# P transposes of three heads with 128 weight columns, and P, its transpose and the small columns in one tile

## The chip, the cores and the metric

The kernel runs on one core of a Trainium2 chip. A core has TensorE (matmuls into PSUM, with weight loads that are instructions of their own), VectorE (DVE), ScalarE (ACT), GpSimd (POOL) and SyncE (SP), which run their own instruction streams and meet through semaphores; DMA queues are filled by SP and POOL. The metric is the device time of one execution in microseconds, as a median over runs. Before the change it is 1793.92 us (three runs, 1793.05 to 1796.88).

## The reference

Two kinds of layer alternate, A, B, A, B, each added to its input after a layer norm. The sequence has 2048 rows of 512; A has 32 heads of 128.

```python
def _A_ref(x, mem0, Wq, Wk, Wv, Wo, seg_len):       # seg_len 32, M = 8 memory rows
    L = M + seg_len
    mask = (idx[:, None] < M) | (idx[:, None] >= idx[None, :])
    mem = mem0
    for s in range(n_seg):                          # 64 segments, one after the other
        h = jnp.concatenate([mem, xs], axis=1)      # 40 rows
        q, k, v = h @ Wq, h @ Wk, h @ Wv            # per head
        p = softmax(where(mask, q @ k.T * scale, -1e9))
        o = (p @ v) @ Wo                            # summed over heads
        mem = o[:, :M, :]                           # memory of the next segment
        outs.append(o[:, M:, :])
def _B_ref(x, w_gate, w_up, w_down):                # 512 -> 1792 -> 512
    return (sigmoid(x @ w_gate) * (x @ w_up)) @ w_down
```

Every segment of A needs the 8 memory rows that the segment before it produced, so A is a chain of 64 steps in each of the two layers.

## The kernel before

**Steps.** The two A layers run as one chain of 70 steps (`emit_step`). In step t, job 0 is segment t of the first A layer and job 1 is segment t - 6 of the second; where both exist (58 steps) the two 40-row segments lie side by side in 80 columns, `LW = 2 * L`. The B layers (`ffn`), the layer norms and the passes that make V run between the steps.

**Inside a step.** The 32 heads go in six groups: four of six heads, one of six and one of two. A "unit" is a set of heads whose P and V are stacked over partitions: the first eight units have three heads (3 x 40 = 120 partitions), the last four have two (80 partitions). So the first four groups have two units of three heads each, the fifth three units of two, the sixth one unit of two. For each group:

1. q and k of three heads at a time (L988, weights of 128 x 128, 80 moving columns), copied from PSUM to `qku` by ACT (L1354).
2. Scores (L1023); DVE adds the mask (L1037), takes the maximum (L1042), subtracts it (L1044); ACT takes the exponential (L1047); DVE sums (L1049), takes the reciprocal (L1051) and multiplies into `pb` (L1054), a bf16 tile of 80 partitions by 6 heads x 40.
3. P is transposed on TensorE, unit by unit (L1067): the weights are the unit's columns of `pb` (120 columns for three heads, 80 for two), the moving operand is the identity (80 columns), and the result lies in PSUM with the unit's heads stacked over 120 or 80 partitions.
4. Head i of each unit is copied ("spread") from PSUM rows 40 i to 40 i + 39 into its own 40 columns of `ptsb`, so that `ptsb` is block diagonal. For i = 0 it is a plain copy; for i = 1 and 2 the copy is multiplied by a column of ones and zeros, `third[i]`, which lies among the small columns. Each copy is on ACT or DVE, whichever the order chose: L1346 and L1354 on ACT, L1348 and L1356 on DVE. L1354 and L1356 are helper lines that make all plain copies of those engines.
5. P times V (L1096), weights `vsb`, moving operand `ptsb`; ACT copies the result to `otsb` (L1354); Wo (L1114) accumulates over the groups, and its first rows become the memory of the next step (L1127, L1132).

**Tiles.** There are three `pb` tiles and three `ptsb` tiles, used in turn. `small` is one tile of 61 float columns: statistics of the layer norms (`lns`), maxima and sums of the softmax (`mx`), the two columns `third` and a constant. In all, seven tiles. `pb` and `ptsb` are cleared once at the start by POOL (L652, L657).

**Order.** A planner (`Planner`) holds every piece of work as a task. The order of the tasks is written out in the file (`SEQUENCE`, and `TURNS` for the turns of `qku`); the planner walks it with estimated durations, puts each task on an engine and a PSUM bank, and the result is issued as it stands. The semaphore waits are not written by hand: the tile framework derives them from the accesses to each tile, and leaves out a wait that an earlier one on the same engine already implies. It makes waits between two engines, and also of an engine on its own earlier instructions. POOL's weight transfers of the B layers (L1208, L1209, L1233) and SP's transfers of V into `vsb` (L956, L968) are tasks of the same order.

Of the kernel before, what the change touches and what calls it, by code (L numbers as in the profile page):

```python
# [13 lines left out]
BF16 = mybir.dt.bfloat16  # L14
F32 = mybir.dt.float32
# [5 lines left out]
P = 128  # L21
MEM = 8
SEG = 32
L = MEM + SEG
LW = 2 * L
# [7 lines left out]
def fview(base, dims):  # L33
    return bass.AP(tensor=base.tensor, offset=base.offset, ap=[tuple(base.ap[0])] + [tuple(d) for d in dims])
# [497 lines left out]
class Kern:  # L532
# [43 lines left out]
    def setup_tiles(self):  # L576
        ctx, tc, nc = self.ctx, self.tc, self.nc
        D, DC, H, HG, F, FC, R = self.D, self.DC, self.H, self.HG, self.F, self.FC, self.R
        HE = H * P
        c = ctx.enter_context(tc.tile_pool(name="c", bufs=1))  # L580
        dr = ctx.enter_context(tc.tile_pool(name="dr", bufs=1, space=bass.MemoryType.DRAM))
        self.scr = [dr.tile([self.NSEG * XS, HE], BF16, name=f"scr{j}") for j in range(2)]
        self.wq = c.tile([P, DC, HE], BF16, name="wq_sb")
        self.wk = c.tile([P, DC, HE], BF16, name="wk_sb")
        self.wv = c.tile([P, DC, HE], BF16, name="wv_sb")
        self.wo = c.tile([P, H, D], BF16, name="wo_sb")
        cst = c.tile([P, P + 2 * L], BF16, name="cst")
        self.ident, self.maskb, self.mask1 = cst[:, 0:P], cst[:, P:P + L], cst[0:L, P + L:P + 2 * L]
        small = c.tile([P, 61], F32, name="small")
        self.negh = small[:, 60:61]  # L590
        self.third = [None, small[:, 58:59], small[:, 59:60]]
        self.lns = [small[:, 10 * i:10 * i + 10] for i in range(4)]
        self.mx = [small[:, 40 + 6 * i:46 + 6 * i] for i in range(3)]
        self.NV = 2
        self.hT = [c.tile([P, DC, 2 * L], BF16, name=f"hT{i}") for i in range(R)]
        self.qku = [c.tile([P, 3, 2, LW], BF16, name=f"qku{i}") for i in range(3)]
        self.vsb = {("A", i): c.tile([P, 2, 1024], BF16, name=f"vsb{i}") for i in range(self.NV)}
        self.vsb.update({("B", i): c.tile([P, 2, 512], BF16, name=f"vsb{self.NV + i}") for i in range(self.NV)})
        self.st = [c.tile([P, HG, L], F32, name=f"st{i}") for i in range(3)]
        self.pb = [c.tile([LW, HG, L], BF16, name=f"pb{i}") for i in range(3)]  # L600
        self.ptsb = [c.tile([P, 17 * L], BF16, name=f"ptsb{i}") for i in range(3)]
        self.otsb = [c.tile([P, HG, 2 * L], BF16, name=f"otsb{i}") for i in range(2)]
        self.hot = fview(self.otsb[1][:, 0, 0:1], [(1, P)])
        self.NX = 6
        self.xs = [c.tile([P, D], BF16, name=f"xs{i}") for i in range(self.NX)]
        self.xa = [c.tile([P, D], BF16, name=f"xa{i}") for i in range(2)]
        self.oxT = [[c.tile([P, DC, P], BF16, name=f"oxT{j}_{i}") for i in range(2)] for j in range(2)]
        self.xn = [c.tile([P, D], BF16, name=f"xn{i}") for i in range(2)]
        self.xnT = [c.tile([P, DC, P], BF16, name=f"xnT{i}") for i in range(1)]
        self.kx = c.tile([P, H, 2, NE], BF16, name="kx")  # L610
        self.xq = dr.tile([self.LAG * P, H * 2 * NE], BF16, name="xq")
        self.hff = [c.tile([P, FC, P], BF16, name=f"hff{i}") for i in range(1)]
        self.th = [c.tile([P, 2, P], F32, name=f"th{i}") for i in range(1)]
        self.xvf = [c.tile([P, DC, P], BF16, name=f"xvf{i}") for i in range(2)]
        self.xvl = [c.tile([P, DC, P], BF16, name=f"xvl{i}") for i in range(3)]
        self.vst = [c.tile([P, 512], BF16, name=f"vst{i}") for i in range(3)]
        self.sst = [c.tile([P, 2, 512], BF16, name=f"sst{i}") for i in range(1)]
        self.NG, self.ND = 3, 3
        self.wg = [c.tile([P, DC, 2 * P], BF16, name=f"wg{i}") for i in range(self.NG)]
        self.wu = [c.tile([P, DC, 2 * P], BF16, name=f"wu{i}") for i in range(self.NG)]  # L620
        self.wd = [c.tile([P, 2, D], BF16, name=f"wd{i}") for i in range(self.ND)]
        pp = ctx.enter_context(tc.tile_pool(name="ps", bufs=1, space=PSUM))
        self.bank = Pool([pp.tile([P, 512], F32, name=f"bank{i}") for i in range(8)], {"bg": 3, "v": 3}, psum=True)
        self.qkp = Pool(self.qku)
        self.vstp = Pool(self.vst)
        self.sstp = Pool(self.sst)
        self.bootp = Pool([fview(w[:, 0, 0:1], [(1, 1024)]) for w in self.wd + self.wg + self.wu])
        self.xnp = Pool(self.xn)
        self.thp = Pool(self.th)
# [281 lines left out]
    def emit_step(self, t):  # L911
        nc, pl = self.nc, self.pl
# [7 lines left out]
        pr = slice(0, ncol)  # L920
        npart = ncol
        nj = len(jobs)
        full = slice(0, LW)
# [9 lines left out]
        if load:  # L933
            for lo, hi in parts:
                w = NE * 2
                pl.add("SP", 430, lambda lo=lo, hi=hi, w=w: nc.sync.dma_start(out=fview(self.kx[:, lo, 0, 0:1], [(1, (hi - lo) * w)]),
                                                                             in_=self.xq[(t - LAG) * P:(t - LAG + 1) * P, lo * w:hi * w]),
# [5 lines left out]
        def s_all(B):  # L943
            return B[:, 0:6 * ncol].rearrange("p (h k) -> p h k", h=6)
# [5 lines left out]
        for j in jobs:  # L950
# [4 lines left out]
            for vh, i, h0, nh in slots if s or not j else ():  # L955
                pl.add("SP", 430, lambda j=j, row=L * i + row + lo, h0=h0, nh=nh, vh=vh, r0=s * XS + lo, nx=nx: nc.sync.dma_start(  # L956
                    out=self.vsb[vh][row:row + nx, j, :], in_=self.scr[j][r0:r0 + nx, h0 * P:(h0 + nh) * P]),
                    r=[("vd", j, b, q, kk) for q in range(lo // 8, (lo + nx) // 8) for kk in range(h0 // 4, (h0 + nh) // 4)] + ([("wo", self.H - 1)] if t == 0 else []),
                    w=[("vx", j, vh, i)], lat=2700.0, nb=nx * 256 * nh, slow=0.9)
# [13 lines left out]
        for g, (heads, us) in enumerate(self.groups):  # L973
            gsz = len(heads)
            hs = slice(0, gsz)
            SB = pl.buf(self.bank)
            for w0 in range(0, gsz, 3):
# [5 lines left out]
                def qk(uh=uh, nh=nh, pq=pq):  # L983
                    for i, h in enumerate(uh):
# [7 lines left out]
                       w=[pq])  # L992
# [21 lines left out]
                for lo, hi in parts:  # L1014
                    if save and pos == hi:
                        w = NE * 2
                        pl.add("SP", 430, lambda lo=lo, hi=hi, w=w: nc.sync.dma_start(out=self.xq[t * P:(t + 1) * P, lo * w:hi * w],
                                                                                     in_=fview(self.kx[:, lo, 0, 0:1], [(1, (hi - lo) * w)])),
# [9 lines left out]
            st, mx = self.st[gi], self.mx[gi]  # L1028
            sm = rs = mx
            bi = self.nxt("pb", 3)  # L1030
            pb = self.pb[bi]
            n = gsz * L
            for idx, j in reversed(list(enumerate(jobs))):
# [4 lines left out]
                    out=st[pj_, hs], in0=s_all(SB)[pj_, hs, L * idx:L * (idx + 1)],  # L1038
# [6 lines left out]
                out=st[pr, hs], in0=st[pr, hs], in1=mx[pr, hs].unsqueeze(2).to_broadcast([npart, gsz, L]), op=ALU.subtract),  # L1045
# [5 lines left out]
            pl.add("DVE", 110, lambda hs=hs, rs=rs, sm=sm: nc.vector.reciprocal(out=rs[pr, hs], in_=sm[pr, hs]), r=[("mx", gi)], w=[("mx", gi)])  # L1051

            def pmul(gsz=gsz, hs=hs, st=st, rs=rs, pb=pb):
                nc.vector.tensor_tensor(out=pb[pr, hs, 0:L], in0=st[pr, hs],  # L1054
                                        in1=rs[pr, 0:gsz].unsqueeze(2).to_broadcast([npart, gsz, L]), op=ALU.mult)

            pl.add("DVE", dve_ns(n), pmul, r=[("st", gi, 0), ("st", gi, 1), ("mx", gi)], w=[("pb", bi)])
            pi = self.nxt("ptsb", 3)
            ptsb = self.ptsb[pi]
            PB = pl.buf(self.bank)  # L1060
            nu = len(us)
            w = gsz // nu

            def ptr(nu=nu, w=w, pb=pb, PB=PB):
                pt = PB[0:w * L, 0:nu * LW // 2].bitcast(BF16)
                for ul in range(nu):
                    nc.tensor.transpose(out=pt[:, ul * LW:(ul + 1) * LW], in_=pb[full, w * ul:w * ul + w, :].rearrange("p i k -> p (i k)"),  # L1067
                                        identity=self.ident[full, full])

            pl.add("PE", nu * mm_ns(LW), ptr, r=[("pb", bi)], w=[PB])  # L1070
            for i in range(w):
                def spread(i=i, nu=nu, ptsb=ptsb, PB=PB):
# [56 lines left out]
        else:  # L1129
            for idx, j in wj:  # L1130
                m = SEG + MEM * j
# [288 lines left out]
```

## Time and profile before

| | |
|---|---|
| timed runs, median (range) | 1793.92 us (1793.05 to 1796.88) |
| profiled execution, its own time | 1789.87 us |
| its span, first to last instruction | 1788.0 us |
| granted TensorE clock | 0.999 |
| P transposes (L1067) | 840 matmuls; 560 with 120 weight columns, 280 with 80 |
| spreads on ACT | 477 (L1346) + 260 (L1354 into `ptsb`) |
| spreads on DVE | 223 (L1348) + 160 (L1356 into `ptsb`) |
| DMA traffic | 273.39 MB, mean 153 GB/s |

In the groups of the profile, a line gives the source line, the engine and operation, output and input tiles, shapes (partitions x elements, or contraction rows * weight columns for TensorE) and the count; then the busy time in us and the mean duration of one in ns; then the engine's idle time in us ahead of these instructions, with what ended most of it. "PE" is matmuls, "PEld" weight loads, which run beside matmuls. A duration of a matmul or load is that of one, with its way through the array; the next one starts long before its end. In a time line, a row gives the start and length in us, the engine, line and operation, the count that was merged, and in brackets the idle time before it and what released it. "SPq" is SP's queue.

### The profile page before, as it was taken

The numbers are of one execution on the slowest core, as the hardware profiler recorded it, in microseconds if no ns is written. First come the engines' busy times: TensorE is split into PE (matmuls) and PEld (weight loads), VectorE is DVE, ScalarE is ACT, GpSimd is POOL, SyncE is SP. The second block draws the span as 40 slices with busy tenths as digits, with TensorE's granted clock in tenths as the row PEclk, the third lists the DMA queues.
The fourth block names the chain that finished last, engine by engine and source line by source line (L and its number), as shares of the span: only waits on it lengthen the run. The fifth ranks groups of instructions, "written<-read, shape, count | busy, mean of one in ns | idle before, by whom it ended". The sixth has DMA issues, their size and how long they took to land.

```text
span 1788.0 us, 91153 instructions
## 1 busy us (share of the span) xinstructions
PE 1752.0 (98%) x39103; PEld 1512.2 (85%) x39311; DVE 1182.3 (66%) x4076; ACT 1179.3 (66%) x3243; POOL 578.6 (32%) x837
## 2 busy tenths in 40 slices
PE   9999999999999999999999999999999999999998
PEld 4588788888888898989888898889888888889886
DVE  3367676776677667766776677667766765667675
ACT  4667777766666666666666666666666766666564
POOL 5412132422333242323324231333325231333432
PEclk9999999999999999999999999999999999999999
DMA  9735354634555463545546454556546454554543
GB/s 340 255 98 141 106 162 131 188 106 141 156 165 159 132 191 109 159 127 166 158 133 194 137 154 111 148 161 167 157 128 197 116 149 120 161 155 135 165 137 100
DMA packets 144752, 273.39 MB, mean 153 GB/s; under 512 B 34306, under 2 KB 82314, under 8 KB 144346
## 3 DMA queue, kind: packets, MB, share of 16 engines
q0 software_dynamic: 56720, 183.22, 35.1%
q1 hardware_dynamic: 87626, 84.31, 16.7%
q8 instruction: 308, 5.05, 1.2%
q14 instruction: 98, 0.80, 0.1%
HBM read 221.78 MB, written 27.07 MB: 139 GB/s over the span
## 4 chain that ended last, share of the span: by engine, by line
PE 89%; ACT 3%; DVE 2%; issue 1%; SPq 1%; DMA 1%; POOL 0%; DVEq 0%; ACTq 0%; POOLq 0%
PE bank L988 32%; PE bank L1114 17%; PE bank L1216 10%; PE bank L902 7%; PE bank L778 6%; PE bank L1023 4%; PE bank L1096 4%; PE bank L1239 4%; PE bank L1067 2%; PE bank L738 1%; DVE st L1037 1%; PE bank L1340 1%; SPq L968 1%; ACT ptsb L1346 1%; PE bank L1184 1%
## 5 line engine op out<-in xcount | busy, mean ns | idle before, releaser
L988 PE MATMUL bank<-hT,wq_sb 128*128 128x80 bf16 (+3 forms) x8960 | 615.5, 198 | 1.2
L988 PE MATMUL bank<-hT,wk_sb 128*128 128x80 bf16 (+3 forms) x8960 | 615.2, 198 | 0.8 <-issue 0.8
L1354 ACT CAST qku<-bank 128x480 bf16<-128x480 f32 (+3 forms) x770 | 380.7, 507 | 215.5 <-PE bank L988 185.1
L988 PEld LDWEIGHTS <-wq_sb 128*128 128x128 bf16 x8960 | 453.4, 99 | 23.3 <-issue 11.7
L988 PEld LDWEIGHTS <-wk_sb 128*128 128x128 bf16 x8960 | 447.0, 99 | 1.0 <-issue 1.0
L1037 DVE TENSOR_TENSOR st<-bank,cst 40x240 f32<-40x240 f32 (+3 forms) x768 | 278.9, 368 | 163.3 <-PE bank L1023 152.6
L1114 PE MATMUL bank<-otsb,wo_sb 128*128 128x80 bf16 (+1 forms) x8960 | 358.6, 198 | 1.6 <-ACT otsb L1354 0.2
L1114 PEld LDWEIGHTS <-wo_sb 128*128 128x128 bf16 x8960 | 336.5, 99 | 13.5 <-issue 0.9
L1209 POOL DMA_DIRECT2D wu<-in_B_w_up_dram x217 | 164.0, 756 | 273.6 <-PE bank L1216 126.5
L1208 POOL DMA_DIRECT2D wg<-in_B_w_gate_dram x217 | 163.9, 756 | 256.4 <-PE bank L1216 181.9
L1354 ACT CAST otsb<-bank 128x480 bf16<-128x480 f32 (+3 forms) x420 | 198.3, 483 | 52.3 <-PE bank L1096 35.4
L1233 POOL DMA_DIRECT2D wd<-in_B_w_down_dram x217 | 153.7, 709 | 207.4 <-PE bank L1023 71.8
L1346 ACT ACTIVATE ptsb<-bank,small 80x160 bf16<-80x160 bf16 (+5 forms) x477 | 169.5, 379 | 27.7 <-PE bank L1067 23.9
L1047 ACT ACTIVATE st<-st 80x240 f32<-80x240 f32 (+3 forms) x420 | 159.7, 383 | 29.0 <-DVE st L1044 25.6
L728 POOL TENSOR_TENSOR small<-small 128x1 f32<-128x1 f32 (+1 forms) x80 | 44.8, 563 | 402.1 <-DVE small L727 400.0
L1216 PE MATMUL bank<-xnT,wg 128*128 128x128 bf16 (+2 forms) x1784 | 172.0, 219 | 0.6
L1216 PE MATMUL bank<-xnT,wu 128*128 128x128 bf16 (+2 forms) x1784 | 171.0, 218 | 0.0
L1049 DVE TENSOR_REDUCE small<-st 80x6 f32<-80x240 f32 (+3 forms) x420 | 151.2, 362 | 24.5 <-ACT st L1047 22.8
L1023 PE MATMUL bank<-qku 128*128 128x80 bf16 (+1 forms) x2240 | 165.4, 198 | 0.7
L1044 DVE TENSOR_TENSOR st<-st,small 80x240 f32<-80x240 f32 (+3 forms) x420 | 154.4, 369 | 3.4
L1054 DVE TENSOR_TENSOR pb<-st,small 80x240 bf16<-80x240 f32 (+3 forms) x420 | 153.8, 369 | 4.2
L1042 DVE TENSOR_REDUCE small<-st 80x6 f32<-80x240 f32 (+3 forms) x420 | 151.8, 363 | 4.3
(104 smaller groups left out, 2405.3 us busy)
## 6 DMA issues: line engine op xcount, KB each, us to landing
wg<-in_B_w_gate_dram POOLq DMA_DIRECT2D x220, 256.0 KB, 4.4
wu<-in_B_w_up_dram POOLq DMA_DIRECT2D x220, 256.0 KB, 4.4
wd<-in_B_w_down_dram POOLq DMA_DIRECT2D x220, 256.0 KB, 4.3
vsb<-scr SPq DMA_DIRECT2D x345, 48.0 KB
vsb<-sst SPq DMA_DIRECT2D x372, 32.0 KB
scr<-vst SPq DMA_DIRECT2D x112, 96.0 KB
vsb<-scr SPq DMA_DIRECT2D x230, 24.0 KB
wv_sb<-in_A_Wv_dram SPq DMA_DIRECT2D x8, 512.0 KB
```

The lines of the kernel that those rows point to most:

```text
L988: nc.tensor.matmul(o_ap, lhsT=W[:, c, h * P:(h + 1) * P], rhs=mv(c), start=(c == 0), stop=(c == DC - 1))
L1023: nc.tensor.matmul(s_all(SB)[:, w0 + i, :], lhsT=fview(qku[:, i, 0, 0:1], [(1, P)]), rhs=qku[:, i, 1, 0:ncol], start=True, stop=True)
L1037: pl.add("DVE", dve_ns(n, True), lambda gsz=gsz, hs=hs, st=st, SB=SB, pj_=pj_, npj_=npj_, mk=mk, idx=idx: nc.vector.tensor_tensor(out=st[p ...
L1044: pl.add("DVE", dve_ns(n), lambda gsz=gsz, hs=hs, st=st, mx=mx: nc.vector.tensor_tensor(out=st[pr, hs], in0=st[pr, hs], in1=mx[pr, hs].uns ...
L1047: pl.add("ACT", act_ns(n), lambda hs=hs, st=st: nc.scalar.activation(out=st[pr, hs], in_=st[pr, hs], func=ACTF.Exp, scale=self.scale), r=s ...
L1054: nc.vector.tensor_tensor(out=pb[pr, hs, 0:L], in0=st[pr, hs], in1=rs[pr, 0:gsz].unsqueeze(2).to_broadcast([npart, gsz, L]), op=ALU.mult)
L1114: nc.tensor.matmul(WB[:, c * ncol:(c + 1) * ncol], lhsT=self.wo[:, h, c * P:(c + 1) * P], rhs=otsb[:, hl, 0:ncol], start=(h == 0 and c == ...
L1208: pl.add("POOL", 760, lambda wg=wg, fs=fs: nc.gpsimd.dma_start(out=wg[:], in_=self.wgv[:, :, fs]), r=[("wo", self.H - 1)], w=[gk] + bt, la ...
L1209: pl.add("POOL", 760, lambda wu=wu, fs=fs: nc.gpsimd.dma_start(out=wu[:], in_=self.wuv[:, :, fs]), r=[("wo", self.H - 1)], w=[uk] + bt, la ...
L1216: nc.tensor.matmul(gu[:, 2 * i + k, 0:n], lhsT=W[:, c, i * P:(i + 1) * P], rhs=xnT[:, c, rw], start=(c == 0), stop=(c == DC - 1))
L1346: nc.scalar.activation(out=dst, in_=src, func=ACTF.Copy, scale=by)
L1354: nc.scalar.copy(out=dst, in_=src)
```

## The change

The weights of a three-head transpose take 128 columns of `pb` in place of 120. The first unit's extra 8 columns are the first 8 of the second unit; the second unit's are 8 columns past the end of the P tile, which is now 248 columns wide and cleared at the start. The transpose writes 128 rows of PSUM, of which the last 8 are read by nothing. Transposes of two heads stay at 80 columns.

The three P tiles, the three `ptsb` tiles and `small` become parts of one tile, `pbt`: first the three `ptsb` of 680 columns, then the three P of 248, then the 61 float columns. The names `pb`, `ptsb`, `mx`, `lns`, `third` now are views of it. The planner's tasks, costs and written order are the same. In the changed file the lines from the tiles on stand 2 or 3 further down (the transposes at L1070, the spreads at L1349, L1351, L1357 and L1359).

```diff
-        small = c.tile([P, 61], F32, name="small")
-        self.negh = small[:, 60:61]
-        self.third = [None, small[:, 58:59], small[:, 59:60]]
-        self.lns = [small[:, 10 * i:10 * i + 10] for i in range(4)]
-        self.mx = [small[:, 40 + 6 * i:46 + 6 * i] for i in range(3)]
...
-        self.pb = [c.tile([LW, HG, L], BF16, name=f"pb{i}") for i in range(3)]
-        self.ptsb = [c.tile([P, 17 * L], BF16, name=f"ptsb{i}") for i in range(3)]
+        np_, nt_ = HG * L + P - 3 * L, 17 * L
+        pbt = c.tile([P, 3 * (np_ + nt_) + 2 * 61], BF16, name="pbt")
+        self.ptsb = [pbt[:, nt_ * i:nt_ * (i + 1)] for i in range(3)]
+        self.pb = [pbt[0:LW, 3 * nt_ + np_ * i:3 * nt_ + np_ * (i + 1)] for i in range(3)]
+        small = pbt[:, 3 * (np_ + nt_):3 * (np_ + nt_) + 2 * 61].bitcast(F32)
+        self.negh = small[:, 60:61]
+        self.third = [None, small[:, 58:59], small[:, 59:60]]
+        self.lns = [small[:, 10 * i:10 * i + 10] for i in range(4)]
+        self.mx = [small[:, 40 + 6 * i:46 + 6 * i] for i in range(3)]
...
             def pmul(gsz=gsz, hs=hs, st=st, rs=rs, pb=pb):
-                nc.vector.tensor_tensor(out=pb[pr, hs, 0:L], in0=st[pr, hs],
+                nc.vector.tensor_tensor(out=pb[pr, 0:gsz * L].rearrange("p (h k) -> p h k", k=L), in0=st[pr, hs],
...
             def ptr(nu=nu, w=w, pb=pb, PB=PB):
-                pt = PB[0:w * L, 0:nu * LW // 2].bitcast(BF16)
+                m = P if w == 3 else w * L
+                pt = PB[0:m, 0:nu * LW // 2].bitcast(BF16)
                 for ul in range(nu):
-                    nc.tensor.transpose(out=pt[:, ul * LW:(ul + 1) * LW], in_=pb[full, w * ul:w * ul + w, :].rearrange("p i k -> p (i k)"),
+                    nc.tensor.transpose(out=pt[:, ul * LW:(ul + 1) * LW], in_=pb[full, w * L * ul:w * L * ul + m],
                                         identity=self.ident[full, full])
```

## The prediction

> **What bounds the kernel now.** I read the page's busy rows, its chain that ended last, then groups of instructions with shapes kept apart, and last the time lines of single engines around one transpose.
>
> ```profile
> span 1788.0 us, 91153 instructions
> PE 1752.0 (98%) x39103; PEld 1512.2 (85%) x39311; DVE 1182.3 (66%) x4076; ACT 1179.3 (66%) x3243; POOL 578.6 (32%) x837
> ...
> PE 89%; ACT 3%; DVE 2%; issue 1%; SPq 1%; DMA 1%; POOL 0%; DVEq 0%; ACTq 0%; POOLq 0%
> ```
>
> TensorE sets the end: 89% of the last chain is its matmuls, and it idles for 1788.0 - 1752.0 = 36 us. So a matmul slot saved is time saved, unless TensorE then stands before an operand. ACT and DVE are two thirds busy, but they stand between TensorE's own steps. The rows of the changed transposes, with their peers:
>
> ```profile
> L988 PE MATMUL bank<-hT,wq_sb 128*128 128x80 bf16 x6656 | 485.7, 202 | 1.1
> ...
> L1096 PEld LDWEIGHTS <-vsb 120*128 120x128 bf16 x1024 | 65.5, 98 | 15.7 <-issue 4.6 <-DMA vsb<-sst 0.3
> L1067 PEld LDWEIGHTS <-pb 80*120 80x120 bf16 x560 | 55.7, 134 | 9.6 <-DVE pb L1054 1.9 <-DVE st L1044 0.4
> ...
> L1096 PEld LDWEIGHTS <-vsb 80*128 80x128 bf16 x512 | 28.9, 98 | 5.5 <-issue 1.0 <-DMA vsb<-scr 0.2
> L1067 PEld LDWEIGHTS <-pb 80*80 80x80 bf16 x280 | 22.2, 118 | 4.2 <-DVE pb L1054 0.9
> ...
> L738 PEld LDWEIGHTS <-xn 128*128 128x128 bf16 x312 | 19.8, 98 | 8.4 <-DVE xn L729 3.2 <-issue 2.1 <-DVE sst L1356 0.4
> ```
>
> The reader is to see the mean of one weight load: 118 ns with 80 columns, 134 with 120, but 98 with 128. It is 98 with 80 rows (vsb) as with 128, and in a transpose too (xn). Now the two time lines of ACT and DVE, where the change adds waits:
>
> ```profile
> 903.45 0.40 DVE L1049 TENSOR_REDUCE small<-st 80x6 f32<-80x240 f32 x1 [0.47 <-ACT st L1047]
> 903.89 0.19 DVE L1051 RECIPROCAL small<-small 80x6 f32<-80x6 f32 x1
> 904.11 0.41 DVE L1054 TENSOR_TENSOR pb<-st,small 80x240 bf16<-80x240 f32 x1
> ...
> 904.91 0.50 DVE L1348 TENSOR_SCALAR ptsb<-bank,small 120x160 bf16<-120x160 bf16 x2
> 905.33 0.22 DVE L1356 COPY ptsb<-bank 40x160 bf16<-40x160 bf16 x1
> ```
>
> ```profile
> 915.87 0.28 ACT L1354 COPY ptsb<-bank 40x160 bf16<-40x160 bf16 x1 [0.32 <-PE bank L1067]
> 916.06 0.67 ACT L1346 ACTIVATE ptsb<-bank,small 120x160 bf16<-120x160 bf16 x2
> ```
>
> The sum, reciprocal and product each read the one before and wait for it: each starts 0.03 to 0.04 us after its predecessor's end. The spreads wait for none of their own engine: the DVE copy starts at 905.33, 0.08 before the pair ahead ends (905.41), and ACT's pair starts at 916.06, 0.09 before the copy ends (916.15).
>
> **Part 1, the wider transposes.** 560 of the 840 P transposes change (groups of six heads; the 280 with 80 columns do not). Nothing is added or removed on TensorE: the built programs hold 78,624 rows in the same order, and only the output's 120 partitions become 128. In the trace, the first of two such transposes is followed by the second after 47.9 ns in the mean (283 pairs), and the second by the next matmul after 50 to 54 (45 or 55 each, where nothing stalls; 51 taken). Matmuls of 80 columns on weights of 128 follow each other after 35.8 (23,234 pairs, almost all 35 or 36). The saving is 280 x (47.9 - 35.8) + 280 x (51 - 35.8) = 3.4 + 4.3 = 7.6 us of TensorE's slots. It is all on the bound engine, but where TensorE stands before a wait afterwards it is given back. I carried the shorter slots forward through the trace's rows (every instruction starts when its engine is free and its semaphores have come, with the durations and least gaps of these rows; the rest stays as recorded): 7.3 us are won and 2.0 go back, about half of them before DMA-filled vsb (L1096), the rest before pb (L1067), qku (L1023) and otsb (L1114). The part is worth **-5.3 us**. From below: nothing, if the fast load is not taken; from above -7.6.
>
> The Trainium skill (TensorE: Matmul & The Clock Gate, LDWEIGHTS and Weight-path perf modes) has a load at columns / 1.2 ns, and about twice as fast with exactly 128 non-fp32 columns. By it the estimate is 560 x (100 - 53) = 26 us saved; the spacing of 48 to 51 ns that the rows show for 120 columns contradicts its 100, and the rows decide.
>
> **Part 2, one tile for P, its transpose and the small columns.** Same instructions on ACT, DVE and SP in the same order, and no wait between two engines changes. But the waits of an engine on itself do. In the built program of before, a spread (L1346, L1348, or the copy into ptsb at L1354 and L1356) is free of its neighbour. In the changed one, 255 spreads on ACT wait for the ACT instruction just ahead, nearly always the group's previous spread, and 81 on DVE likewise; 41 and 19 more wait for the one before that, which is over by then, and cost nothing. What it costs:
> - DVE: instructions without such a wait start 75 to 80 ns before their predecessor's end, with it 34 ns after (125 pairs L1037 to L1042, 111 pairs L1051 to L1054). 34 + 78 = 112 ns, and 81 x 112 = 9.1 us of DVE.
> - ACT: spread after spread starts 102 ns before the end (96 pairs L1346 to L1346). No ACT instruction of before waits for its direct predecessor closely enough to show the price. From below: it starts as the predecessor ends, 102 ns. From above: the largest gap between a producer's end and its consumer here, ACT to TensorE, 50 ns, so 152. Nearest are DVE to itself (34), DVE to ACT (33) and ACT to DVE (31); I take 34, so 136 ns, and 255 x 136 = 34.7 us of ACT.
> - Given back: 171 separate wait instructions on ACT vanish, because later instructions need not repeat the wait (76 on copies to otsb). A copy behind such an instruction starts up to 92 ns after TensorE's end, without it 37. This is within the sum below.
>
> Of 43.8 us on the two engines only what arrives late at TensorE counts. P·V (L1096) is first: in 338 of its groups, the spread was there for a median of 253 ns before it had to be, but for under 105 in a quarter. 161 groups get a longer chain of spreads, by one or two of these prices. Held against each group's own margin, 49 of them come late by 4.9 us together. That is the first order alone. Queued behind the spreads on ACT are the copies to otsb (Wo, L1114, waits), to qku (scores, L1023) and the exponentials (L1047, whose sum and product DVE makes for L1067); DVE's own next steps lie behind its spreads. Carried forward in the same way, with 34 ns on both, ACT's waits alone give +9.9 us, DVE's alone +2.0, both +11.9. Together with part 1 TensorE stands longer by 8.6 at L1096 behind spreads, 3.1 at L1114, 3.0 at L1067, 2.5 at L1023, and 1.1 before DMA-filled vsb; it wins 7.3 by spacing and about 3.5 because a stall leaves later ones shorter; with 0.4 of small ones, **+7.9 us**. With ACT and DVE at 50 ns it is +12.2, at 0 ns +2.2.
>
> The Trainium skill (VectorE: DVE Perf Modes, The DRAIN you can't avoid) holds that between chained DVE operations "the semaphore costs nothing extra here". By that sentence the sum would be part 1 alone, -5.3 us. The time line above shows 34 ns after the end against 78 before it, so the measurement decides for a price.
>
> **What has one answer.** The three memsets of pb get 8 of 240 columns more (301 ns each, so 10 ns, in the first 7 us, POOL off the chain): nothing. POOL's weight transfers and SP's keep their order and waits; POOL's wait for TensorE (181.9 us of it before wg) and move with it. The output in PSUM rows 120 to 127 is read by none.
>
> **The sum.** The profiled execution took 1789.87 us for a span of 1788.0; + 7.9 = 1797.8. The median of the three timed runs is 1793.92, 4.05 higher, so I forecast 1793.92 + 7.9 = **1801.8 us**. About 0.2% (3.6 us) either way can't be told from no change.
>
> **Rivals.**
> - *The waits hide and the slots are kept (faster).* For it: ACT idles a third of the time, and TensorE's recorded idle before L1096 for ACT's ptsb is small. Against it: a quarter of the margins at L1096 is under 105 ns, less than one wait's price. -5.3 gives 1788.6. It decides from an own-engine price of about 80 ns (start 20 ns before the end), where the carried sum crosses zero; below that it is faster.
> - *The change doesn't do what it says.* The second transposes start 240 bytes into a P tile, and the tiles now lie 496 bytes apart; every 128-column load of the trace starts at a rounder address. If the load stays slow, +11.9 and 1805.8 remain; with 128/120 of the slow slot, 560 x 3.3 ns = 1.9 more, 1807.7.
> - *No visible change.* Price about half: sum between -3.6 and +3.6, 1790 to 1797.5.
> - *The waits cost more.* At 60 ns after the end the carried sum is +16.8, 1810.7; stalls grow faster than the price, since more margins are used up.
>
> **How the numbers follow.** Chances: the likeliest, 0.48; waits hidden 0.17; slow load 0.10; no visible change 0.13; dearer waits 0.12. Slower is 0.48 + 0.10 + 0.12 = 0.70, same 0.13, faster 0.17. The likeliest alone spans 1798 to 1806 (price 15 to 50 ns). The range reaches from 1790, which keeps "no change" and leaves most of "faster" out, to 1811, the dearer waits.
>
> **What would show it.** After the change: the weight load of L1067 at about 98 ns instead of 134 and the two transposes in 0.07 us instead of 0.12; spreads that start 0.03 us after the one ahead instead of 0.08 to 0.10 before it; more idle of TensorE before L1096 put down to ACT's and DVE's ptsb (before: 0.6 + 0.2 us in its waits), and before L1114 and L1067. I am wrong if spreads still overlap, if the load stays over 130 ns, or if both hold but idle of TensorE doesn't grow.

## The result

The changed kernel took 1797.64 us in the median (20 runs), the kernel before 1793.07 beside it (20 runs): 1.0031 times as long, or 5.5 us more (95% intervals [1.0021, 1.0041] and [3.8, 7.4]). Differences in us are taken from such ratios unless it says otherwise; the two medians alone give 4.6. A second series gave 1.0027 [1.0012, 1.0042]. The forecast was 1801.8 us, +7.9, in a range of 1790 to 1811: the direction is right, and the size too large, by 2.4 us in the difference and by 4.2 in the time.

**The profile after.** Busy rows and the chain that ended last, from the page of the changed kernel:

```profile
span 1798.9 us, 91186 instructions
...
PE 1765.5 (98%) x39311; PEld 1504.5 (84%) x39311; DVE 1189.3 (66%) x4076; ACT 1197.1 (67%) x3243; POOL 578.8 (32%) x837
...
PE 87%; ACT 4%; SPq 2%; DMA 2%; DVE 1%; issue 1%; POOL 0%; DVEq 0%; ACTq 0%; POOLq 0%
```

TensorE's share of the last chain went from 89% to 87%, ACT's from 3% to 4%. ACT has the same 3,243 instructions, but is busy for 17.8 us more (1179.3 before), because instructions that used to overlap now follow each other. PE's own busy row must not be compared: the trace of before lacks 208 matmul records (39,103 of 39,311), this one none. Nor does it show TensorE's standing: the changed kernel idles for 1798.9 - 1765.5 = 33 us by this row, less than the 36 of before, because a record of about 200 ns covers several slots of 36. Single executions also scatter by several microseconds (those of before in one series lie between 1790.5 and 1802.4), so the 10.9 us between the two profiled spans are no measure of the change; the medians are.

Weight loads with shapes kept apart (count, busy us, mean ns of one, then idle time ahead), and the matmuls of the changed transposes:

```profile
L1099 PEld LDWEIGHTS <-vsb 120*128 120x128 bf16 x1024 | 66.9, 97 | 28.6 <-issue 14.0 <-DMA vsb<-sst 2.4 <-DVE pbt L1351 0.2
...
L1070 PEld LDWEIGHTS <-pbt 80*128 80x128 bf16 x560 | 40.4, 99 | 11.6 <-DVE pbt L1056 3.4 <-DVE st L1046 0.4
...
L1070 PEld LDWEIGHTS <-pbt 80*80 80x80 bf16 x280 | 22.2, 118 | 4.6 <-DVE pbt L1056 1.9
```

```profile
L1070 PE MATMUL bank<-cst,pbt 80*128 80x80 bf16 x560 | 66.2, 200 | 0.8 <-DVE pbt L1056 0.7
```

The load of a three-head transpose takes 99 ns in place of 134, and that of the unchanged 80-column transpose 118 as before. TensorE's time line at one such place, first before, then after:

```profile
904.58 0.29 PE L1067 MATMUL bank<-cst,pb 80*120 80x80 bf16 x2
904.70 0.28 PE L1023 MATMUL bank<-qku 128*128 128x80 bf16 x3
904.82 0.31 PE L988 MATMUL bank<-hT,wq_sb 128*128 128x80 bf16 x4
```

```profile
909.32 0.24 PE L1070 MATMUL bank<-cst,pbt 80*128 80x80 bf16 x2
909.39 0.27 PE L1025 MATMUL bank<-qku 128*128 128x80 bf16 x3
909.50 0.31 PE L990 MATMUL bank<-hT,wq_sb 128*128 128x80 bf16 x4
```

From start to start the two transposes take 0.07 us in place of 0.12, and the three score matmuls behind them 0.11 in place of 0.12. So the first half of the change does what it says. The second half shows in the idle time ahead of the P·V loads: 28.6 us in place of 15.7. It also shows in the time lines of ACT and DVE (start and length in us), here around the same work that the prediction quoted of before:

```profile
920.60 0.29 ACT L1357 COPY pbt<-bank 40x160 bf16<-40x160 bf16 x1 [0.26 <-PE bank L1070]
920.92 0.81 ACT L1349 ACTIVATE pbt<-bank,pbt 120x160 bf16<-120x160 bf16 x2
```

```profile
909.16 0.41 DVE L1225 SCALAR_TENSOR_TENSOR hff<-th,bank 128x256 bf16<-128x256 f32 x1
909.60 0.63 DVE L1351 TENSOR_SCALAR pbt<-bank,pbt 120x160 bf16<-120x160 bf16 x2
910.26 0.23 DVE L1359 COPY pbt<-bank 40x160 bf16<-40x160 bf16 x1
```

ACT's pair now starts at 920.92, 0.03 after the copy ends (920.89). Before, it started 0.09 ahead of that end. The pair itself takes 0.81 in place of 0.67, since its second spread waits for its first. DVE's pair takes 0.63 in place of 0.50, and the copy behind it starts 0.03 after its end in place of 0.08 before.

Over all spreads that follow another directly, counted in the traces (start minus the predecessor's end, median):

| | before | after, with the new wait | after, without one |
|---|---|---|---|
| ACT | -102 ns | +32 ns (255 cases, 31 to 33) | -102 ns |
| DVE | -77 ns | +35 ns (81 cases, 33 to 36) | -77 ns |

**Where TensorE stands.** Its waits in the changed kernel (us in total, times, longest); of the P·V lines, all are shown that have 0.5 us or more:

```profile
PE bank L1099 <- DMA vsb<-sst: 4.4, 5, 1.7
...
PE bank L1099 <- ACT pbt L1349: 2.4, 3, 1.8
PE bank L1099 <- issue: 2.0, 2, 1.2
PE bank L1099 <- DMA vsb<-scr: 1.7, 2, 0.9
...
PE bank L1117 <- ACT otsb L1357: 0.9, 3, 0.5
PE bank L1070 <- DVE pbt L1056: 0.7, 2, 0.4
PE bank L1099 <- ACT pbt L1357: 0.5, 2, 0.3
```

```profile
PEld L1099 <- issue: 15.4, 30, 1.9
...
PEld L1070 <- DVE pbt L1056: 5.3, 20, 0.5
...
PEld L1099 <- DMA vsb<-sst: 2.4, 3, 0.9
```

The largest entry, 15.4 us before P·V's loads (5.6 before), has no releaser: "issue" is waiting for nothing that this view shows. To name it I took each place where two weight loads start over 70 ns apart and asked which result, of all that the built program makes this load or the matmul just ahead of it wait for, came last. Where ACT or DVE had finished it less than 130 ns earlier, the gap, less a regular slot of 36 ns, is put down to them:

| TensorE behind ACT's and DVE's results, us (gaps) | before | after | change again | waits only | 128 columns only |
|---|---|---|---|---|---|
| P·V, behind spreads | 4.0 (22) | 16.3 (74) | 15.5 (75) | 15.5 (71) | 5.0 (23) |
| Wo, behind `otsb` (ACT) | 3.5 (24) | 6.9 (38) | 7.2 (39) | 6.8 (37) | 4.0 (27) |
| transposes, behind P (DVE) | 6.2 (28) | 10.0 (49) | 10.1 (49) | 9.3 (45) | 6.9 (32) |
| scores, behind `qku` (ACT) | 7.1 (35) | 9.4 (49) | 9.5 (51) | 8.7 (46) | 7.4 (35) |
| sum | 20.8 | 42.6 | 42.3 | 40.3 | 23.3 |

The last two columns are experiments below. The change adds some 21 us of such standing, over half of it before P·V, where it falls on about 50 more gaps. The growth of "issue" before P·V in the waits view, 9.8 us, fits into the 12.3 us found there; no other cause for it was seen, but the two were not matched gap by gap.

The table leaves out P·V's waits for V. By the waits view, the matmuls and loads of P·V wait for the transfers into `vsb` for 2.7 us in the kernel before and 8.9 in the changed one (8.1 in the second run). The same sum is 4.6 with the waits only, 5.1 with 128 columns only, 2.0 in the layout control below, and 7.3 with 124 columns, which has neither the waits nor the shorter slots. So this growth can't be put down to the change with any certainty.

### The profile page after: what moved, and what is told of

It is laid out like the page before. It is cut to its first block, busy times and chain, and to the rows that moved or that the text cites. A ratio compares the mean times of both kernels' runs of the same rounds, so it can differ in the third digit from the quotient of the medians.

```text
span 1798.9 us, 91186 instructions
## 1 busy us (share of the span) xinstructions
PE 1765.5 (98%) x39311; PEld 1504.5 (84%) x39311; DVE 1189.3 (66%) x4076; ACT 1197.1 (67%) x3243; POOL 578.8 (32%) x837
## 4 chain that ended last, share of the span: by engine, by line
PE 87%; ACT 4%; SPq 2%; DMA 2%; DVE 1%; issue 1%; POOL 0%; DVEq 0%; ACTq 0%; POOLq 0%
PE bank L990 31%; PE bank L1117 16%; PE bank L1219 9%; PE bank L904 7%; PE bank L780 6%; PE bank L1242 5%; PE bank L1099 4%; PE bank L1025 4%; SPq L970 2%; PE bank L1070 2%; ACT pbt L1349 2%; DMA vsb<-sst 1%; DMA vsb<-scr 1%; PE bank L740 1%; PE bank L1343 1%
## 5 line engine op out<-in xcount | busy, mean ns | idle before, releaser
L1357 ACT CAST qku<-bank 128x480 bf16<-128x480 f32 (+3 forms) x770 | 380.4, 507 | 209.9 <-PE bank L990 177.3
L1357 ACT CAST otsb<-bank 128x480 bf16<-128x480 f32 (+3 forms) x420 | 197.8, 482 | 55.7 <-PE bank L1099 39.7
L1349 ACT ACTIVATE pbt<-bank,pbt 80x160 bf16<-80x160 bf16 (+5 forms) x477 | 177.7, 381 | 29.0 <-PE bank L1070 19.9
L730 POOL TENSOR_TENSOR pbt<-pbt 128x1 f32<-128x1 f32 (+1 forms) x80 | 45.0, 564 | 403.7 <-DVE pbt L729 401.7
L1051 DVE TENSOR_REDUCE pbt<-st 80x6 f32<-80x240 f32 (+3 forms) x420 | 151.6, 363 | 31.8 <-ACT st L1049 28.7
L1046 DVE TENSOR_TENSOR st<-st,pbt 80x240 f32<-80x240 f32 (+3 forms) x420 | 154.6, 370 | 3.4
L1056 DVE TENSOR_TENSOR pbt<-st,pbt 80x240 bf16<-80x240 f32 (+3 forms) x420 | 153.9, 369 | 4.2
L1044 DVE TENSOR_REDUCE pbt<-st 80x6 f32<-80x240 f32 (+3 forms) x420 | 151.9, 363 | 4.3
```

The costliest lines, as they stand in the source:

```text
L1046: pl.add("DVE", dve_ns(n), lambda gsz=gsz, hs=hs, st=st, mx=mx: nc.vector.tensor_tensor(out=st[pr, hs], in0=st[pr, hs], in1=mx[pr, hs].uns ...
L1056: nc.vector.tensor_tensor(out=pb[pr, 0:gsz * L].rearrange("p (h k) -> p h k", k=L), in0=st[pr, hs], in1=rs[pr, 0:gsz].unsqueeze(2).to_broa ...
L1349: nc.scalar.activation(out=dst, in_=src, func=ACTF.Copy, scale=by)
L1357: nc.scalar.copy(out=dst, in_=src)
```

## The experiments

**The theory.** Two opposite effects of known place: the 128-column loads shorten TensorE's slots, and the new waits of ACT and DVE on themselves make TensorE stand behind spreads; the second is larger. **Rivals:** the loads bring nothing; the time comes from the new placement of the tiles in memory, not from waits; only one of the two engines matters; or the two parts do not add.

How the waits arise was seen in the built programs. With `ptsb` and the float columns in one tile, the 255 and 81 waits are there; with P and the float columns in one tile, or with `ptsb` and P in one tile and the float columns in another, there are none, and the waits between engines are the same in all. Of these three, only the last was also run, below. So one part can be had without the other.

**The change again**, beside the next three on the same chip. No edit.

> The changed kernel once more, beside the parts that are taken from it. Measured 1.0031 of before. Theory (the engines' waits on themselves cost more than the faster weight loads save): again 1.002 to 1.005, and the parts below add up to it. Rival (the layout of the one tile costs it): the same here, but the narrow kernel with the small columns apart is slower too.

Measured: 1801.73 us against 1796.03, ratio 1.0027 [1.0012, 1.0042]. The result repeats.

**The waits alone.** One tile as in the change, the transposes at 120 columns:

```diff
-                m = P if w == 3 else w * L
+                m = w * L
```

> One tile pbt as in the change, but the transposes take 120 columns again: the waits of ACT and DVE on themselves without the faster loads. Theory: +8 to +12 us over before (the carried sum had +11.9), ratio 1.0045 to 1.0067, weight loads at 134 ns. Rival 1 (the loss comes from the earlier transposes, which bring TensorE to V that is still on its way): about 0, ratio 1.000. Rival 2 (the layout): the same as the change, 1.003.

Measured: 1805.87 us, ratio 1.0058 [1.0039, 1.0078], or +10.4 us. The load is back at its old mean:

```profile
L1070 PEld LDWEIGHTS <-pbt 80*120 80x120 bf16 x560 | 55.5, 134 | 10.1 <-DVE pbt L1056 2.8 <-DVE st L1046 0.4
```

Without the wider transposes the changed kernel would be slower still. The standing behind ACT and DVE is 40.3 us, nearly that of the full change: it comes with the tile, not with the columns.

**The 128 columns alone.** The float columns stay a tile of their own; `ptsb` and P share one, so P lies where the change puts it:

```diff
-        pbt = c.tile([P, 3 * (np_ + nt_) + 2 * 61], BF16, name="pbt")
+        pbt = c.tile([P, 3 * (np_ + nt_)], BF16, name="pbt")
+        small = c.tile([P, 61], F32, name="small")
...
-        small = pbt[:, 3 * (np_ + nt_):3 * (np_ + nt_) + 2 * 61].bitcast(F32)
```

> The transposes take 128 columns, P and its transpose share one tile, and the small float columns are a tile of their own again. In the built program no engine waits more than before. Theory: the saving alone, -3 to -6 us, ratio 0.9967 to 0.9983; spreads overlap again by about 100 ns on ACT and 77 on DVE. Rival 1 (earlier transposes only move the wait to V): 1.000 or above. Rival 2 (layout of P and its transpose in one tile): 1.002 or above.

Measured: 1789.59 us, ratio 0.9958 [0.9940, 0.9975], or -7.5 us (-6.4 by the medians): faster than both kernels, and by somewhat more than the 3 to 6 us expected. Both rivals wanted 1.000 or more: that the earlier transposes only move the wait to V does not hold. It ran again in the next series:

> The kernel with the small columns apart once more, beside the two that add waits to it. Measured 0.9958 of before. Both theories: 0.995 to 0.998.

Measured: 1788.41 against 1795.79, ratio 0.9956 [0.9941, 0.9972], -7.9 us. Its loads (by shapes) are the short ones, and its spreads (time line of ACT) overlap again:

```profile
L1070 PEld LDWEIGHTS <-pbt 80*128 80x128 bf16 x560 | 40.8, 99 | 11.0 <-DVE pbt L1056 2.3 <-DVE st L1046 0.4
```

```profile
917.04 0.29 ACT L1357 COPY pbt<-bank 40x160 bf16<-40x160 bf16 x1 [0.30 <-PE bank L1070]
917.23 0.67 ACT L1349 ACTIVATE pbt<-bank,small 120x160 bf16<-120x160 bf16 x2
```

The pair starts at 917.23, 0.10 before the copy ends, and takes 0.67, as before the change.

**The layout alone**, as a control: that edit and 120 columns (`m = w * L`).

> The layout control: as the kernel with the small columns apart, but 120 columns in the transposes, so neither part of the change is left but other addresses. Theory: 0, ratio 0.9985 to 1.0015. Rival 2 (layout): 1.003 or more.

Measured: 1793.47 us, ratio 0.9996 [0.9982, 1.0010]. The standing sums to 21.3 us (20.8 before). Moving P and `ptsb` into one tile costs nothing that can be measured, so that rival falls. By the medians of this series the 128 columns are worth 4.1 us beside the waits (1805.87 to 1801.73) and 3.9 without them (1793.47 to 1789.59), so there is no sign that the two parts do not add.

**ACT's waits alone and DVE's waits alone.** To the kernel with 128 columns alone, a wait of each spread for the group's previous spread on the same engine is added, in groups of two or more units over two segments, where the change has them. This is ACT's; DVE's has `("DVE",)`:

```diff
+        last = {}
...
-                def spread(i=i, nu=nu, ptsb=ptsb, PB=PB):
+                def spread(i=i, nu=nu, ptsb=ptsb, PB=PB, nj=nj):
...
+                if tk.fn.__name__ == "spread" and tk.fn.__defaults__[1] * tk.fn.__defaults__[4] >= 4 and tk.on in ("ACT",):
+                    key, ins = (tk.on, id(tk.fn.__defaults__[3])), nc.cur_bb.bb.instructions[-1]
+                    if key in last:
+                        self.tc.add_manual_dep(ins, last[key], self.SYNC, reason="spreads one after another")
+                    last[key] = ins.name
```

> Small columns apart, 128 columns, and ACT's spreads given just the waits on ACT that the change gave them (255 on the instruction just ahead), DVE none. Theory (each of ACT's 255 waits costs 134 ns of ACT, 34 us in all, and ACT's waits carry most of the loss: +9.9 of +11.9 us in the carried sum): 1.0005 to 1.003 of before, which is 8 to 11 us over the kernel with the small columns apart. Rival (the few waits on DVE decide, because DVE also makes P and has the longer chain): at most 4 us over it, 0.996 to 0.998.

> The same with DVE's waits alone (81 on the instruction just ahead, 112 ns each, 9 us of DVE). Theory: +2 us over the kernel with the small columns apart (1 to 4), 0.996 to 0.998 of before. Rival (DVE's waits decide): 8 us or more over it, 1.000 or above.

Measured, both beside the repeated 128-column kernel (0.9956): ACT's waits 1797.99 us, 1.0019 [1.0005, 1.0032]; DVE's 1791.20, 0.9977 [0.9960, 0.9993]. So ACT's waits cost 11.3 us by the ratios (9.6 by the medians), DVE's 3.8 (2.8). ACT's alone take away the whole gain of the columns. The intervals of the DVE kernel and of the one without waits overlap, but both are taken against the same runs of before. Held against each other directly, 8 of the 12 runs with DVE's waits are longer than the longest of the 8 without (1789.51), so the cost is above zero, though its size is loose. First the time line of ACT in the kernel with ACT's waits, then that of DVE in the kernel with DVE's:

```profile
924.84 0.29 ACT L1358 COPY pbt<-bank 40x160 bf16<-40x160 bf16 x1 [0.35 <-PE bank L1070]
925.16 0.82 ACT L1350 ACTIVATE pbt<-bank,small 120x160 bf16<-120x160 bf16 x2
```

```profile
912.10 0.63 DVE L1352 TENSOR_SCALAR pbt<-bank,small 120x160 bf16<-120x160 bf16 x2
912.76 0.23 DVE L1360 COPY pbt<-bank 40x160 bf16<-40x160 bf16 x1
```

Each engine shows the starts of the changed kernel (0.03 after the end; pairs of 0.82 and 0.63), with `small` a tile of its own. The standing behind spreads at P·V follows the engine: ACT's part is 11.4 us with ACT's waits and 3.3 with DVE's; DVE's is 2.4 with ACT's and 6.2 with DVE's; without either it is 2.6 and 2.4. (The profiled executions of these two kernels were the longest of their 12, 1803.12 and 1796.43 us, some 5 us above their medians, so their sums may be high.) Which waits there are decides the loss, not the tile that brings them. The two prices sum to 15.1 us, while both together cost 10.4 (waits alone) or 12.4 to 13.1 (the two series of the change against the 128-column kernel). That a stall behind one engine hides part of the other's is possible but not shown: the intervals, about 3 us either way, leave room for a plain sum.

**124 columns**, to see whether the count of exactly 128 matters or just a wider transpose: the 128-column kernel with

```diff
-                m = P if w == 3 else w * L
+                m = P - 4 if w == 3 else w * L
```

> Small columns apart, and the three-head transposes take 124 weight columns. Theory (only exactly 128 columns load fast, and a slower load takes columns / 2.4 ns of a slot): loads of about 136 ns, slots of 52 ns instead of 50, 0 to +2 us over before, 0.999 to 1.002. Rival (a wider load as such is faster, or the gain lies elsewhere in the new form of the transpose): loads near 98 to 110 ns and 0.996 to 0.998.

Measured: 1797.98 us, ratio 1.0008 [0.9994, 1.0022]. Loads by shapes:

```profile
L1070 PEld LDWEIGHTS <-pbt 80*124 80x124 bf16 x560 | 56.6, 136 | 9.4 <-DVE pbt L1056 1.9 <-DVE st L1046 0.4
```

136 ns, a little over the 134 of 120 columns, and no gain in time. The step lies between 124 and 128. The Trainium skill (TensorE: Matmul & The Clock Gate, Weight-path perf modes) says that the fast load is on when the number of weights is 128 and the type is not fp32; these rows agree, also for 80 contraction rows and a transpose.

The slots behind these loads, from the traces (mean spacing of matmul starts, ns):

| weight columns | first transpose to second | second to the next matmul | that one to the matmul after it |
|---|---|---|---|
| 120 (before; waits only; layout alone) | 46.5 to 46.7 | 51.2 to 51.4 | 52.3 to 52.4 |
| 124 | 47.5 | 53.0 | 52.4 |
| 128 (change; 128 columns only) | 40.4 | 35.4 | 43.9 to 44.1 |

The third slot lies between two unchanged matmuls and still shrinks by 8.4 ns. The next slot behind it is 40.3 to 40.5 in all of these kernels, and the slots ahead of the transposes do not change either (spacings over 70 ns, which are stalls, are left out).

## Why the prediction was right, and where its sizes were off

**Part 1, slots.** The prediction expected both slots at 35.8 ns. The second came to 35.4, the first only to 40.4. With the slots recounted in the same way in all kernels (46.5 and 51.2 before), these two save 280 x 6.1 + 280 x 15.8 = 1.7 + 4.4 = 6.1 us in place of 7.6. But the prediction left out the third slot of the table, which saves 280 x 8.4 = 2.4 us more. The saving in slots is 8.5 us: the first slot was taken too short, the third was put at nothing, and the stated bound of -7.6 was no bound. Entering a run of transposes seems to cost 4 to 5 ns whatever the weights: the unchanged 80-column transposes have 41 for the first slot and 36 for later ones, on loads of 118 ns, in the trace of before already. By them the first slot could have been taken right. They show the third as well: behind a group of three of them, whose loads stay slow, it is 51.6 ns in the trace of before and 51.7 with 128 columns for the others.

**Part 1, time.** Forecast -5.3 us with bounds of 0 and -7.6. Measured -7.5 [-10.8, -4.5] and -7.9 [-10.6, -5.0]; against the layout control the medians alone give -3.9. The forecast lies within both intervals, so the difference is not resolved. Some giving back is there, but its size is not settled: 2.0 us were forecast in all. In the two profiled runs of that kernel, TensorE stands 2.5 and 1.8 us longer behind ACT and DVE alone, and all weight-load spacings over 70 ns, less a slot of 36 each, sum to 6.6 and 3.6 us more than before, whatever ended them.

**Part 2, the price.** Taken: 34 ns after the end on both engines. Measured: 32 on ACT, 35 on DVE. The rows of DVE behind its own results and between DVE and ACT were a good guide to ACT behind itself, which the trace of before could not show.

**Part 2, what reaches TensorE.** Forecast +11.9 us for both engines, measured +10.4 [7.0, 14.0] for the waits alone. By engine, +9.9 and +2.0 were forecast and 11.3 and 3.8 measured (9.6 and 2.8 by the medians), on top of the 128-column kernel; the order is right, and the forecast for DVE is low, within what the intervals leave. The split by place holds too: forecast 8.6 us more at P·V behind spreads, 3.1 at Wo, 3.0 at the transposes, 2.5 at the scores; the change shows 12.3 (11.5 in the second run), 3.4 (3.7), 3.8 (3.9) and 2.3 (2.4). The term sized too small is P·V. The first-order estimate there, 49 groups late by 4.9 us, came close in the count (52 more gaps; whether they are the same groups was not looked at) and is far too small in the size. The prediction's reason, that a late spread also delays what is queued behind it on ACT, fits this but was not tested alone.

**The sum.** Between the two profiled executions, 21.8 us more standing behind ACT and DVE (forecast 17.2, and 1.1 behind the transfers into `vsb`) and 8.5 us of slots won (7.3 carried) leave 2.4 us given back as the net of all the rest (3.5 forecast, because a stall leaves later ones shorter) to make +10.9, the difference of the spans. The giving back can be seen in the waits alone, where no slot is won: weight-load spacings of up to 70 ns sum to 1312.7 us against 1317.7, and 81 more spacings, some 3 us of regular slots, have moved into the longer class; about 2 us remain.

The timed runs show +5.5, though. Of the two profiled executions, that of before was short for its kernel (1789.87 against a median of 1793.07) and that of the change long (1800.80 against 1797.64). The two offsets are 3.2 us each, and together they make the difference between 10.9 and the medians' 4.6. So the forecast of +7.9, made from one short execution, stands between what the profiles and what the timed runs show, and of its error of 2.4 us no single term can be named as the cause. Put right, standing that was 3 to 4 too low and giving back that was 1.1 too high would raise the forecast, and slots that were 1.2 too low would reduce it: the better terms give +10.9, which is further from the timed runs. That the forecast came as close as it did is in part luck; the mechanism, its two signs and its order of sizes are not.

**The rivals.** "The waits hide" is false: the held spreads start 32 and 35 ns after the end, where the carried sum crosses zero at a start 20 ns before it, and the waits alone cost 10.4 us. "The change doesn't do what it says": all 560 loads take 95 to 103 ns, though by the layout of the tile the starts of the units differ by 16, 32 and 48 bytes modulo 64. "No visible change" and "dearer waits" fail by the price, which is neither half nor 60 ns. By the time alone, "no visible change" (up to +3.6) fails only narrowly: the first interval begins at 3.8 us, and that of the second series, at 2.2, does not exclude it.

The sentence of the Trainium skill that the prediction weighed (VectorE: DVE Perf Modes, The DRAIN you can't avoid: "the semaphore costs nothing extra here") does not carry over to this case: the wait moves a DVE spread from 77 ns before its predecessor's end to 35 after it, 112 ns, and DVE's 81 waits are put at 3.8 us. The same section says that a next instruction which is not held starts earlier; the -77 ns agree with that.

One thing in the description of the kernel needs a correction. A spread of head i covers rows 0 to 40 i + 39, and the column `third[i]` blanks the rows of the other heads. The spreads of a group still write different columns, so no result depends on the waits. Why the framework can't keep them apart once the float columns share the tile was not settled.

## What to carry to other kernels

Before tiles of different uses are merged, compare the built programs' waits, those of an engine on itself included: here a few hundred waits that no data needs cost more than the wider loads won, and leaving one small float tile apart (1788.4 to 1789.6 us) kept the gain and lost the cost. Price such a wait as the gap it makes plus the overlap it ends (134 ns on ACT, 112 on DVE), and count what is queued behind it, not only its own reader. Padding a weight load to exactly 128 columns paid here even with unused columns; padding to 124 did not.

## What the runs showed that was not expected

- The first transpose of a run has a slot of 40 to 41 ns, with 128 columns and with 80, though the loads take 99 and 118 ns; the later ones have 35 to 36. The reason is open.
- The recorded length of a weight load does not give its slot: 118 ns with 80 columns goes with 36 (later transposes), 134 ns with 120 columns with 46.5 to 51.2, 99 ns with 128 columns with 35.4.
- A faster weight load also shortens a slot between later matmuls whose own loads are unchanged: the second matmul after the transposes follows the first after 44 ns in place of 52. Behind slow loads of 80, 120 and 124 columns it is 52. The reason is open.
- The 128-column load kept its 99 ns with weights whose starts differ by 16, 32 and 48 bytes modulo 64.
- Waits on spreads are largely missing by name from the waits view: by the program's own semaphores TensorE stands 16.3 us behind spreads at P·V in the changed kernel, while the view puts 3.4 us of its matmuls' waits under ACT's and DVE's spreads, and 15.4 us of its loads' under "issue".
